# A recomputed opening schedule for batch 0: GpSimd held from H to dH, weight low parts on two engines, batch 1's first sums moved ahead of the main loop

## The chip, the core and the metric

The kernel runs on one core of a Trainium2 chip. A core has five engines that each work through their own queue in order: TensorE (PE, matrix products, with a separate row PEld for its weight loads), VectorE (DVE), ScalarE (ACT), GpSimd (POOL) and SyncE (SP, here only a DMA queue). Engines wait for one another by semaphores. The metric is the device time of one execution in microseconds, lower is better. Three timed runs of the kernel before gave 304.07, 304.18 and 304.26 us.

## The reference

Four batches of 12480 rows with 128 channels, 32 inducing vectors, and a gated feed-forward of width 2048 behind the attention:

```python
def mab(q, kv):
    s = scale * (q @ kv.transpose(0, 2, 1))
    s = s - s.max(-1, keepdims=True)
    a = np.exp(s)
    a /= a.sum(-1, keepdims=True) + 1e-09
    return a @ kv
h = mab(I, x)                  # 32 x 128 for each batch
y = mab(x, h)                  # 12480 x 128 for each batch
...
u = y @ w_in                   # 128 -> 2048
g = u * np.clip(u + 3.0, 0.0, 6.0) / 6.0
out = g @ w_out                # 2048 -> 128
```

Every output row depends on the whole batch only through `h`, a 32 x 128 matrix. Once `h` (called H below) is known, the kernel turns both weight matrices into small tables, and each row is finished with these tables.

## The kernel before

**Stages.** A batch is cut into seven groups of rows: six of 2048 (16 tiles of 128) and a rest of 192. Stage A goes over the groups: x is loaded by DMA issued from POOL (`load_x`, L140), cast to bf16 (L299), transposed on PE (L310), copied from PSUM (`xT`, L317), multiplied with the inducing vectors (scores, L323), exponentiated on ACT (L333), and the weighted sums of x are accumulated on PE in one PSUM bank (`hnd`, `a_agg`, L360), while DVE adds up the weights (`dacc`, `a_sum`, L375 and L377). Stage C follows: H is `hnd` over its denominator (L464), HT its transpose (L474), then HTb and HTl (its bf16 high and low part, L479 and L484), W, Wd and dH (sums and differences of its columns, L489 to L502). From these come the table G of `w_in` with H (`gp`, L514, three products for each of 16 blocks; the third one needs `w_in_l`, the low part of `w_in`), hs and L and BD (L567 to L603), and for batch 0 sixteen products dpm of `w_in` with dH (L613), each squared to a bf16 tile sq (L623 to L628) and multiplied with `w_out` into one PSUM bank cp (L639), from which Cq is read (L652 and L654). Stage B, the main loop, goes over 25 chunks of a batch: for each chunk features TF (bp, L816, and an exponential, L829) and TD (L844, which needs a tile d spread over the partitions by a DMA from SP, L804), the product with BD that opens the output bank (L855), 16 products with Cq (L874), and on DVE the scaling and evacuation (L894).

**What overlaps.** Batch 0 has nothing to hide behind: its stages A and C are laid out by a table, `ORDER`, of some 200 tokens. A token issues one step, and its position fixes the order on that step's engine; `:A`, `:D`, `:P` name ACT, DVE or POOL, and `:o` or `:f` the PSUM pool (`psO` with two banks, `psF` with five; a third pool `psH` has one bank, for `hnd`). The other tokens that matter here are: `wi` (cast of half of `w_in` on ACT), `wl` (an eighth of `w_in_l`, `w_low`), `wo` (cast of a quarter of `w_out`), `bk`, `bT`, `bx`, `bs`, `ba` (batch 1's group 0: casts, transposes, copies, scores, exponential), `pe` (the two products ep and pp), `e` and `dk` (their exponentials), `spread` (the DMAs of d), `dp`, `q`, `C` (dpm, square, product into cp), `G` (four blocks of gp), `by` and `bg` (new, see the change). A square is done on ACT in one step, or, where the block is in `BY_DVE`, on DVE in two (copy from PSUM, multiply). The token `made` puts a one-element copy on POOL that reads W, so POOL's queue stands still until W is there; the token `held` does the same with d of chunk 3 and then issues the four loads of batch 1's groups 1 to 4.

**Batch 1 in the loop.** From the first chunk of the main loop on, `a_units` (L379) deals the steps of the next batch's stage A out over the loop at fixed positions between the groups of four products (`bg`, L1049). Batch 1's group 0 is cast, transposed, scored and exponentiated in the opening already; its weighted sums (two halves of eight products) and its `dacc` copy are issued by `a_units` in the loop, and behind the second half `load_next` (L163) issues the load of batch 1's group 5.

Of the kernel before, what the change touches and what calls it, by code (L numbers as in the profile page):

```python
# [9 lines left out]
FP32 = mybir.dt.float32  # L10
# [19 lines left out]
AHEAD = 6  # L30
CASTLEAD = 1.6
SUMG = 5
BY_DVE = (1, 4, 7, 10)


ORDER = """
half s0:o k1.1:P k1.2 k1.0:D a0 warm1:o T1.0:o T1.1:f y0 xT1.0:A g0.0 xT1.1:D g0.1 k2.0:P k2.2
k2.1:D s1:f dx5 T2.0:f a1 dx6 T2.1:f xT2.0:D g1.0 xT2.1:A y1 g1.1 k3.1:D k3.2 dx10 k3.0:D s2:f
T3.0:o dwi a2 T3.1:o xT3.0:A g2.0 y2 dwo g2.1 xT3.1:D s3:f k4.0:D k4.2 k4.1:D warm2:f T4.0:f a3
T4.1:f xT4.0:D g3.0 xT4.1:A y3 g3.1 k5.0:D k5.1:P k5.2 s4:f k6:D T6:f T5.0:o xT6:D a4 T5.1:o  # L40
xT5.0:D s6:f g4.0 xT5.1:A y4 g4.1 dred a6 s5:f bk2:A bk3:P a5 bk0:P bT1:f bk1:P n5 wi0 n6 den
bT0:f dall rD bx1:A g5.0 wl1 bx0:D g5.1 wl2 wi1 g6 bs:f wl3 H htp:o ba wl0 HT HTb wo1:A Wd wl6
warm3:o pe1:of wo0:A HTl pe0:ff wo2:P dk1 G0 dH e1 G1 dk0 wl7 dp9:f e0 dp7:f spread0 dp5:o W q9
dp15:f dp1:o q7 wl4 q5 bp0.0:f C9 q15 made wl5 bp1.0:f C5 q1 C7 dp11:o TF1.0 held dp10:f dp14:f
TF0.0 G2 q10 C1 q14 G3 dp0:f wo3:A hs bp0.1:o q0 C10 C14 C15 dp6:f cmax TF0.1 dp2:f dp8:f C0 q2
TD0 L0:f q8 L1 q6 C8 dp4:o L q11 C2 C6 q4 dp12:f dp13:f dp3:f q12 lt:f sp0:o q13 BD C12 q3 C4
C13 nf0 C11 C3 bp1.1:o Cq rp0:f TF1.1 rp1 r0 warm1:f
""".split()


# [17 lines left out]
def kernel(  # L68
# [8 lines left out]
    nc = tc.nc  # L77
# [31 lines left out]
    with ExitStack() as es:  # L109
# [82 lines left out]
            at = slice(h * F // 2, (h + 1) * F // 2)  # L192
            nc.scalar.copy(w_in_b[:, at], w_in_r[h][:, :].bitcast(FP32))

        def w_low(i):
            lo, hi = i * 256, (i + 1) * 256
            t, at = w_in_r[2 * lo // F], lo % (F // 2)
            nc.gpsimd.tensor_sub(w_in_l[:, lo:hi], t[:, at : at + 256].bitcast(FP32), w_in_b[:, lo:hi])
# [154 lines left out]
        def a_agg(b, g, h):  # L353
            t0, p, n = groups[g]
            st = S[b]
            lo, hi = (0, n // 2) if h == 0 else (n // 2, n)
            if g == 0 and h == 0:
                st["hnd"] = psH.tile([P, 512], FP32, name="hnd", tag="hnd")
            for i in range(lo, hi):
                nc.tensor.matmul(  # L360
                    st["hnd"][:M, :C],
                    lhsT=st[("a1", g)][:p, i * M : (i + 1) * M],
                    rhs=xs[(b, g)][:p, i, :],
                    start=(g == 0 and i == 0),
                    stop=(g == NGR - 1 and i == n - 1),
                )
            if h:
                load_next(b, g)

        def a_sum(b, g):  # L370
# [8 lines left out]
        def a_units(b, when):  # L379
# [121 lines left out]
            nc.vector.tensor_sub(st["dH"][:, 0], shifted(HT, 0, 1, 0), shifted(HT, 2, 0, 2))  # L501
            nc.vector.tensor_sub(st["dH"][:, 1], shifted(HT, 1, -1, 0), shifted(HT, 10, 0, 2))  # L502
# [413 lines left out]
        def first(kind, ix, how):  # L916
# [45 lines left out]
                while held:  # L962
                    load_x(1, held.pop(0))
            elif kind == "made":
                gate("made", S[0]["W"][:, 0, 0, 0:1])
            elif kind == "wi":
                w_in_cast(i)
            elif kind == "wo":
                w_out_cast(i, eng)
            elif kind == "wl":  # L970
                w_low(i)
            elif kind == "bk":
                a_cast(1, 0, ((eng, i, i + 1),))
            elif kind == "bT":
# [4 lines left out]
                a_scores(1, 0, at)  # L979
            elif kind == "ba":  # L980
                a_exp(1, 0)
            elif kind == "dred":
                c_sum(0)
            elif kind == "HTb":
# [338 lines left out]
```

## Time and profile before

| | |
|---|---|
| median of three runs | 304.18 us (304.07 to 304.26) |
| the profiled execution's own time | 304.03 us |
| its span, first to last instruction | 302.3 us |
| PE busy | 285.4 us (94%) |
| DVE, ACT, POOL busy | 237.3, 228.8, 119.0 us |
| H written (L464) | 28.52 to 28.86 us |
| first product with Cq (L874) | 44.73 us |

The opening table covers the time from 0 to 44.7 us, and the main loop the rest. An engine row that is busy says only that the engine had an instruction under way; a PE row of 100% in a stretch means that no gap is seen between its matmuls there. In the timelines each row is a start, a duration, an engine, the source line, the operation with output and inputs, and a count of merged instructions; in square brackets stand the idle time before it and what ended it.

### The profile page before, as it was taken

The page shows a single profiled execution, that of the slowest core. Times are in us where ns is not written, and L with a number is a line of the kernel's source. Part 1 is how long each engine was busy: PE and PEld are TensorE (multiplying, and loading weights), DVE is VectorE, ACT ScalarE, POOL GpSimd, SP SyncE. Part 2 cuts the span into 40 slices and gives each one's busy share as a digit, 9 for nine tenths or more (in the row PEclk, how much of TensorE's full clock was granted, in tenths as well). Part 3 has the DMA queues.
Part 4 walks back from the last instruction along what each step waited for, and adds up shares of the span by engine and source line. Part 5 has one row for each costly group of instructions (what it writes and reads, how often), then busy time and mean ns, then how long its engine had stood idle before and what let it go on. Part 6 is the DMA issues. An engine that isn't in the chain of part 4 may idle for free. (4 is left out here: it accounts for less than half of the span.)

```text
span 302.3 us, 9818 instructions
## 1 busy us (share of the span) xinstructions
PE 285.4 (94%) x3973; PEld 229.0 (76%) x3973; DVE 237.3 (79%) x494; ACT 228.8 (76%) x427; POOL 119.0 (39%) x234
## 2 busy tenths in 40 slices
PE   8989899999998999999998999998799999999992
PEld 3777478988887787887887878777677777777881
DVE  1766898878998588879896787787787787888892
ACT  3788968777878988769698888665687787777760
POOL 8367435411029996000297744000777760000000
PEclk9999999999999999999999999999999999999998
DMA  6999498899867459988657515436553666666753
GB/s 213 426 391 242 104 330 315 274 356 327 297 197 241 130 169 299 360 236 296 194 126 255 177 26 193 161 97 199 187 172 75 189 203 202 197 214 217 218 207 114
DMA packets 25281, 66.69 MB, mean 221 GB/s; under 512 B 3184, under 2 KB 18320, under 8 KB 19344
## 3 DMA queue, kind: packets, MB, share of 16 engines
q1 hardware_dynamic: 18784, 38.36, 39.4%
q0 software_dynamic: 6448, 27.66, 28.6%
q8 instruction: 32, 0.52, 0.7%
q14 instruction: 17, 0.14, 0.1%
HBM read 27.67 MB, written 25.56 MB: 176 GB/s over the span
## 5 line engine op out<-in xcount | busy, mean ns | idle before, releaser
L829 ACT ACTIVATE TF<-bp 128x512 bf16<-128x512 f32 (+1 forms) x200 | 115.7, 589 | 33.7 <-PE bp L816 19.7
L874 PE MATMUL op<-Cq,TF 128*128 128x128 bf16 (+1 forms) x784 | 104.6, 221 | 0.0
L874 PE MATMUL op<-Cq,TD 128*128 128x128 bf16 (+1 forms) x784 | 102.5, 219 | 0.0
L894 DVE TENSOR_TENSOR os<-op,r_all 128x512 f32<-128x512 f32 x96 | 65.9, 687 | 22.8 <-PE op L874 22.2
L844 DVE TENSOR_TENSOR TD<-TF,d 128x1024 bf16<-128x1024 bf16 (+1 forms) x100 | 75.7, 757 | 2.6 <-ACT TF L829 1.5
L816 PE MATMUL bp<-xT,W 128*128 128x512 bf16 (+1 forms) x200 | 74.9, 375 | 2.1 <-DVE nf_all L730 1.0
L874 PEld LDWEIGHTS <-TF 128*128 128x128 bf16 (+1 forms) x784 | 55.1, 98 | 24.4 <-issue 12.9
L874 PEld LDWEIGHTS <-TD 128*128 128x128 bf16 (+1 forms) x784 | 60.4, 98 | 0.2 <-issue 0.2
L855 PE MATMUL op<-BD,nf 128*128 128x512 f32 (+1 forms) x100 | 52.5, 525 | 0.0
L299 ACT CAST xb<-xr 128x512 bf16<-128x512 f32 (+1 forms) x66 | 43.3, 663 | 6.6 <-DMA xr<-in_x_dram 6.6
L317 DVE COPY xT<-pt 128x1024 bf16<-128x1024 bf16 (+1 forms) x50 | 30.3, 609 | 15.3 <-PE pt L310 14.0
L544 POOL TENSOR_TENSOR dg<-G 128x256 f32<-128x256 f32 x48 | 40.6, 846 | 0.0
L543 POOL TENSOR_TENSOR dg<-G 128x256 f32<-128x256 f32 x48 | 31.8, 662 | 13.5 <-ACT sq L551 8.8
L541 POOL COPY gate<-TD 128x1 bf16<-128x1 bf16 x48 | 11.7, 244 | 61.2 <-DVE TD L844 60.5
L551 ACT ACTIVATE sq<-dg 128x512 bf16<-128x512 f32 x48 | 30.2, 632 | 3.0 <-POOL dg L544 2.9
L310 PE MATMUL pt<-ident_b,xb 128*128 128x128 bf16 x392 | 30.4, 219 | 1.7 <-DVE xb L299 1.2
L360 PE MATMUL hnd<-xr,a 128*32 128x128 f32 x384 | 30.9, 226 | 0.0
L310 PEld LDWEIGHTS <-xb 128*128 128x128 bf16 x392 | 23.3, 98 | 5.5 <-DVE xb L299 2.4
L759 PE MATMUL rp<-one,nf 128*128 128x4 f32 (+1 forms) x100 | 26.2, 264 | 0.0
L795 ACT ACTIVATE dk<-pp 128x512 bf16<-128x512 f32 (+1 forms) x28 | 15.6, 557 | 13.6 <-PE pp L781 13.6
L360 PEld LDWEIGHTS hnd<-xr,a 128*32 128x32 f32 x384 | 24.7, 109 | 1.2 <-issue 0.8
L639 PE MATMUL cp<-w_out_b,sq 128*128 128x128 bf16 x256 | 23.7, 219 | 1.9 <-ACT TF L829 1.3
(126 smaller groups left out, 398.5 us busy)
## 6 DMA issues: line engine op xcount, KB each, us to landing
xr<-in_x_dram POOLq DMA_DIRECT2D x23, 1024.0 KB, 7.6
out_dram<-os SPq DMA_DIRECT2D x23, 1024.0 KB, 4.1
d<-dk SPq DMA_DIRECT2D x96, 128.0 KB, 4.4
xr<-in_x_dram POOLq DMA_DIRECT2D x2, 512.0 KB, 4.7
w_in_r<-in_moe_w_in_dram POOLq DMA_DIRECT2D x2, 512.0 KB, 9.7
w_out_r<-in_moe_w_out_dram POOLq DMA_DIRECT2D x4, 256.0 KB, 10.4
out_dram<-os SPq DMA_DIRECT2D x4, 256.0 KB, 3.5
xl<-in_x_dram POOLq DMA_DIRECT2D x4, 96.0 KB, 4.3
```

The costliest lines, as they stand in the source:

```text
L299: eng(xb[:p, lo:hi, :], xs[(b, g)][:p, lo:hi, :].bitcast(FP32))
L310: nc.tensor.transpose(pt[:, (i - lo) * p : (i - lo + 1) * p], xb[:p, i, :], ident_b[:p, :p])
L317: eng(S[b][("xT", g)][:, lo * p : hi * p], pt[:, : (hi - lo) * p])
L360: nc.tensor.matmul(st["hnd"][:M, :C], lhsT=st[("a1", g)][:p, i * M : (i + 1) * M], rhs=xs[(b, g)][:p, i, :], start=(g == 0 and i == 0), st ...
L543: nc.gpsimd.tensor_sub(dg[:, 0], stepped(G2, jb, 0, 1, 0), stepped(G2, jb, 2, 0, 2))
L544: nc.gpsimd.tensor_sub(dg[:, 1], stepped(G2, jb, 1, -1, 0), stepped(G2, jb, 10, 0, 2))
L816: nc.tensor.matmul(st[("bp", c, k)][:, :w], lhsT=st["W"][:, k].rearrange("p m i -> p (m i)"), rhs=st[("xT", g)][:, j * w : (j + 1) * w],)
L829: nc.scalar.activation(st[("x", c)][:, k, :w], bp[:, :w], ACT.Exp, scale=scale)
L844: nc.vector.tensor_mul(u[:, :, :w], t[:, :, :w], d[:, :w].unsqueeze(1).to_broadcast([P, 2, w]))
L855: nc.tensor.matmul(op[:p, : S_ * C], lhsT=st[("nf", g)][:R, j * p : (j + 1) * p], rhs=st["BD"][:R, : S_ * C], start=True, stop=False, skip ...
L874: nc.tensor.matmul(op[:p, s * C : (s + 1) * C], lhsT=T[k][:, s * p : (s + 1) * p], rhs=st["Cq"][:, k, :], start=False, stop=(s == S_ - 1 a ...
L894: nc.vector.tensor_mul(ot[:p, j * S_ : (j + 1) * S_, :], op[:p, : S_ * C].rearrange("p (s c) -> p s c", c=C), r_all[:p, b, c, :S_].unsquee ...
```

## The change

`ORDER` is replaced as a whole. Beside the new order of the steps, these things differ:

- The squares on DVE are blocks 2, 6, 11 (three) where they were 1, 4, 7, 10 (four).
- `w_low` takes an engine: parts 0, 7, 1 and 4 go to DVE (part 0 ahead of H, part 7 between H and HT, parts 1 and 4 between HT and dH), parts 2, 3, 5 and 6 stay on POOL.
- The gate `made` reads the last half of dH, where it read W. Ahead of it POOL has parts 2 and 3; behind it parts 5 and 6 and then `held`. POOL's share of the `w_out` casts (`wo2`) goes to ACT, so ACT has all four.
- `bg` (batch 1's group 0 weighted sums, two halves) and `by` (`a_begin` and the `dacc` copy for it) are issued in the opening: the products between the transpose of H and `pe0`, the copy behind W. In the loop only `load_next(1, 0)` is left of that unit.
- Batch 0's gp takes a bank of `psF` (`G0:f`), since the bank of `hnd` is in use by batch 1's sums.
- `pe1` and `dk1` come much later, so that SP gets four spreads behind `dk0` and the other two behind `dk1`, where it got all six at once.
- `c_tail`, which writes Cq in two instructions, is the same text in both.

```diff
-BY_DVE = (1, 4, 7, 10)
+BY_DVE = (2, 6, 11)
 ORDER = """
-half s0:o k1.1:P k1.2 k1.0:D a0 warm1:o T1.0:o T1.1:f y0 xT1.0:A g0.0 xT1.1:D g0.1 k2.0:P k2.2
-k2.1:D s1:f dx5 T2.0:f a1 dx6 T2.1:f xT2.0:D g1.0 xT2.1:A y1 g1.1 k3.1:D k3.2 dx10 k3.0:D s2:f
-T3.0:o dwi a2 T3.1:o xT3.0:A g2.0 y2 dwo g2.1 xT3.1:D s3:f k4.0:D k4.2 k4.1:D warm2:f T4.0:f a3
-T4.1:f xT4.0:D g3.0 xT4.1:A y3 g3.1 k5.0:D k5.1:P k5.2 s4:f k6:D T6:f T5.0:o xT6:D a4 T5.1:o
-xT5.0:D s6:f g4.0 xT5.1:A y4 g4.1 dred a6 s5:f bk2:A bk3:P a5 bk0:P bT1:f bk1:P n5 wi0 n6 den
-bT0:f dall rD bx1:A g5.0 wl1 bx0:D g5.1 wl2 wi1 g6 bs:f wl3 H htp:o ba wl0 HT HTb wo1:A Wd wl6
-warm3:o pe1:of wo0:A HTl pe0:ff wo2:P dk1 G0 dH e1 G1 dk0 wl7 dp9:f e0 dp7:f spread0 dp5:o W q9
-dp15:f dp1:o q7 wl4 q5 bp0.0:f C9 q15 made wl5 bp1.0:f C5 q1 C7 dp11:o TF1.0 held dp10:f dp14:f
-TF0.0 G2 q10 C1 q14 G3 dp0:f wo3:A hs bp0.1:o q0 C10 C14 C15 dp6:f cmax TF0.1 dp2:f dp8:f C0 q2
-TD0 L0:f q8 L1 q6 C8 dp4:o L q11 C2 C6 q4 dp12:f dp13:f dp3:f q12 lt:f sp0:o q13 BD C12 q3 C4
-C13 nf0 C11 C3 bp1.1:o Cq rp0:f TF1.1 rp1 r0 warm1:f
+half s0:o k1.0:P k1.2 k1.1:D a0 warm2:o T1.0:o T1.1:f y0 xT1.0:A g0.0 xT1.1:D g0.1 k2.1:P k2.2
+s1:f k2.0:D dx5 a1 T2.0:f dx6 T2.1:f y1 xT2.0:A g1.0 xT2.1:D g1.1 k3.0:P k3.2 k3.1:D s2:f dx10
+T3.0:o a2 dwi T3.1:o xT3.0:D g2.0 xT3.1:A y2 dwo g2.1 s3:f k4.1:D k4.2 k4.0:D warm3:f T4.0:f a3
+T4.1:f xT4.0:D g3.0 xT4.1:D g3.1 k5.1:P k5.2 s4:f k5.0:D y3 a4 T5.0:f k6:A T5.1:o y4 xT5.0:A
+g4.0 xT5.1:D g4.1 bk3:A bk2:P T6:o s5:f xT6:D bk1:A bk0:P bT1:f a5 dred s6:f bT0:f a6 wi0 n5
+bx1:D g5.0 bx0:D wl2:P wi1 n6 den g5.1 rD wl0:D g6 wo0:A bs:f dall wl3:P H ba htp:o wl7:D HTb HT
+wo1:A bg0 wl1:D HTl wo2:A Wd bg1 wl4:D wo3:A dH pe0:of G0:f W e0 made dp14:f dp4:f wl5:P dk0
+dp0:f dp11:o by G1 q14 spread0 dp6:o q11 wl6:P G2 q0 C14 q4 bp1.1:f C0 dp7:f TF1.1 q6 C11 dp12:f
+q7 dp3:o q12 held G3 C7 q3 C6 hs C12 bp0.1:f C3 bp0.0:f TF0.1 pe1:of TF0.0 cmax dp8:o TD0 dp5:f
+dk1 dp10:f C4 dp1:f q5 L0:f q10 C5 L1 e1 C10 q1 dp2:f L dp15:f q8 lt:o q2 C1 q15 dp13:f C8 dp9:f
+q13 C15 BD sp0:o q9 C13 C2 nf0 C9 bp1.0:f Cq rp0:f TF1.0 rp1 r0
 """.split()
...
-        def w_low(i):
+        def w_low(i, eng):
...
-            nc.gpsimd.tensor_sub(w_in_l[:, lo:hi], t[:, at : at + 256].bitcast(FP32), w_in_b[:, lo:hi])
+            eng.tensor_sub(w_in_l[:, lo:hi], t[:, at : at + 256].bitcast(FP32), w_in_b[:, lo:hi])
...
-            if h:
+            if h and (b, g) != (1, 0):
                 load_next(b, g)
...
-                if g == 0:
+                if g == 0 and b > 1:
                     us.append((0.0, CASTLEAD + 0.1, lambda: a_begin(b)))
...
                 late = [lambda g=g: summed(g, 0), lambda g=g: summed(g, 1)]
+                if (b, g) == (1, 0):
+                    late = [lambda: load_next(1, 0), lambda: None]
...
-        def c_G3(b, lo, hi):
+        def c_G3(b, lo, hi, how="f"):
...
-                st["gp"] = (psF if b else psH).tile([P, 512], FP32, name="gp", tag="fb" if b else "hnd")
+                st["gp"] = bank(how, [P, 512], FP32, "gp")
...
             elif kind == "made":
-                gate("made", S[0]["W"][:, 0, 0, 0:1])
+                gate("made", S[0]["dH"][:, 1, 1, 0, 0:1])
...
             elif kind == "wl":
-                w_low(i)
+                w_low(i, nc.vector if how == "D" else nc.gpsimd)
...
+            elif kind == "bg":
+                a_agg(1, 0, i)
+            elif kind == "by":
+                a_begin(1)
+                a_sum(1, 0)
...
                 b_dk(0, i)
-                if i and ("d", 0) in S[0]:
+                if i and "spread" in S[0]:
                     spread_rest()
             elif kind == "spread":
                 for c in range(4):
                     b_spread(0, c)
+                S[0]["spread"] = True
                 if ("dk", 1) in S[0]:
                     spread_rest()
...
             elif kind == "G":
-                c_G3(0, 4 * i, 4 * i + 4)
+                c_G3(0, 4 * i, 4 * i + 4, at)
```

## The prediction

> **What bounds the kernel now.** I read the page first, then the busy times by stretch, then the timelines of DVE, ACT, PE and POOL from H (28.86 us) to the first product with Cq (44.73 us).
>
> ```profile
> PE 285.4 (94%) x3973; PEld 229.0 (76%) x3973; DVE 237.3 (79%) x494; ACT 228.8 (76%) x427; POOL 119.0 (39%) x234
> 20.00:30.00 10.00, 9.09 (x168) 7.82 (x165) 6.85 (x15) 8.56 (x14) 6.53 (x10) 1.00 1.35 287
> 30.00:40.00 10.00, 8.67 (x125) 5.57 (x121) 9.13 (x15) 8.56 (x18) 5.33 (x11) 1.00 0.49 114
> 40.00:50.00 10.00, 10.00 (x126) 7.81 (x123) 8.22 (x19) 7.80 (x17) 2.79 (x4) 1.00 1.05 403
> 50.00:60.00 10.00, 10.00 (x165) 9.03 (x163) 9.04 (x15) 7.36 (x14) 5.14 (x9) 1.00 0.73 236
> ```
>
> PE is busy for 94% of the span and shows no gap from 40 to 60 us, so in the main loop a PE instruction taken away is time taken away. From 30 to 40 us it isn't PE: it has 1.3 us of gaps there (8.67 of 10 us), and DVE is the fullest engine. The DVE timeline says why:
>
> ```profile
> 28.52 0.34 DVE L464 TENSOR_SCALAR H<-hnd,rD 32x128 f32<-32x128 f32 x1 [0.39 <-PE hnd L360]
> 29.19 0.22 DVE L474 COPY HT<-htp 128x64 f32<-128x64 f32 x1 [0.34 <-PE htp L469]
> 29.45 0.73 DVE L495 TENSOR_TENSOR Wd<-HT 128x32 bf16<-128x32 f32 x1
> 30.11 0.63 DVE L484 TENSOR_TENSOR HTl<-HT,HTb 128x32 bf16<-128x32 f32 x1
> 30.66 0.94 DVE L501 TENSOR_TENSOR dH<-HT 128x256 bf16<-128x256 f32 x1
> 31.53 0.89 DVE L502 TENSOR_TENSOR dH<-HT 128x256 bf16<-128x256 f32 x1
> 32.34 0.41 DVE L489 TENSOR_TENSOR W<-HT 128x256 bf16<-128x256 f32 x1
> 33.09 0.69 DVE L625 COPY d<-dpm 128x512 f32<-128x512 f32 x1 [0.35 <-PE dpm L613]
> ...
> 34.61 0.69 DVE L625 COPY d<-dpm 128x512 f32<-128x512 f32 x1
> ...
> 43.90 0.56 DVE L652 TENSOR_SCALAR Cq<-cp 128x384 bf16<-128x384 f32 x1 [0.26 <-PE cp L639]
> 44.37 0.34 DVE L654 TENSOR_SCALAR Cq<-cp,half_of 128x128 bf16<-128x128 f32 x1
> ```
>
> From HT on, DVE goes from one instruction to the next; its waits of note are 0.35 us for the first dpm and 0.26 us for the last product into cp. A square costs it 34.61 - 33.09 = 1.52 us, copy and multiply together. And four instructions are slower than their like, as the views by tile show (least, median and longest duration in ns over the four batches):
>
> ```profile
> L495 DVE TENSOR_TENSOR Wd<-HT x4: 184/186/734, 29.5 to 206.3; 128x32 bf16<-128x32 f32 x4
> L484 DVE TENSOR_TENSOR HTl<-HT,HTb x4: 193/193/629, 30.1 to 205.8; 128x32 bf16<-128x32 f32 x4
> L489 DVE TENSOR_TENSOR W<-HT x4: 411/420/421, 32.3 to 205.9; 128x256 bf16<-128x256 f32 x4
> L198 POOL TENSOR_TENSOR w_in_l<-w_in_r,w_in_b x8: 659/670/846, 26.9 to 33.0; 128x256 bf16<-128x256 f32 x8
> ```
>
> Wd and HTl take 734 and 629 ns in batch 0 where the median is 186 and 193; dH takes 943 and 885 ns for a shape that W does in 411. These four run while POOL makes low parts (26.9 to 33.0 us); W ran as POOL waited for it. So POOL's work costs DVE 0.55 + 0.44 + 0.53 + 0.47 = 1.99 us on the way to the first dpm. ACT and PE, meanwhile, wait in turn:
>
> ```profile
> 26.73 1.02 ACT L317 COPY xT<-pt 128x1024 bf16<-128x1024 bf16 x1
> ...
> 28.98 0.60 ACT L333 ACTIVATE a<-s 128x512 fp32r<-128x512 f32 x1 [0.28 <-PE s L323]
> ...
> 31.66 0.60 ACT L795 ACTIVATE dk<-pp 128x512 bf16<-128x512 f32 x1
> ...
> 32.88 1.57 ACT L628 ACTIVATE sq<-dpm 128x512 bf16<-128x512 f32 x3
> ...
> 38.98 2.06 ACT L628 ACTIVATE sq<-dpm 128x512 bf16<-128x512 f32 x4 [0.86 <-PE dpm L613]
> 41.55 1.57 ACT L628 ACTIVATE sq<-dpm 128x512 bf16<-128x512 f32 x3 [0.50 <-PE dpm L613]
> ```
>
> ```profile
> 32.47 1.24 PE L613 MATMUL dpm<-dH,w_in_b 128*128 128x512 bf16 x5 [0.69 <-DVE dH L502]
> ...
> 37.67 0.84 PE L639 MATMUL cp<-w_out_b,sq 128*128 128x128 bf16 x12 [0.46 <-DVE sq L626]
> ...
> 44.73 0.28 PE L874 MATMUL op<-Cq,TF 128*128 128x128 bf16 x2
> ...
> 48.11 0.67 PE L360 MATMUL hnd<-xr,a 128*32 128x128 f32 x8
> ...
> 49.54 0.67 PE L360 MATMUL hnd<-xr,a 128*32 128x128 f32 x8
> ```
>
> ```profile
> L816 PE MATMUL bp<-xT,W 128*128 128x512 bf16 (+1 forms) x200 | 74.9, 375 | 2.1 <-DVE nf_all L730 1.0
> L360 PE MATMUL hnd<-xr,a 128*32 128x128 f32 x384 | 30.9, 226 | 0.0
> ```
>
> ACT stands 0.86 and 0.50 us for dpm, because PE in front of these dpm stands 0.46 us for a square of DVE (37.67). The last square ends at 41.55 + 1.57 = 43.12, and 1.61 us later, with the last product into cp and Cq, comes the first product at 44.73. The opening is thus bounded by DVE, with ACT close behind.
>
> **The change part by part.** *POOL held from H to dH.* Without low parts on POOL, Wd, HTl and the two halves of dH fall to 186, 193 and twice 411 ns: -1.99 us of DVE.
>
> *Low parts on DVE.* No such instruction on DVE is in the trace. Nearest below is W (two inputs from SBUF, 256 elements, 0.41 us), nearest above dH beside a busy POOL (0.94 us). Parts 1 and 4 stand between HT and dH with POOL held, so W's price holds: +0.82 us (up to 1.89). Part 7 falls into the 0.34 us that DVE waits for the transpose in front of HT and overhangs by 0.07; part 0 falls into the 0.39 us in front of H, beside POOL's parts 2 and 3, and may push H by 0.5 us if it is slowed like dH.
>
> *One square less on DVE*: -1.52 us. ACT takes it for 0.49 us (four squares in 2.06 us, one alone 0.60).
>
> *The new dacc copy* behind W. Its row in the loop:
>
> ```profile
> 48.79 0.41 DVE L375 COPY dacc<-a 128x512 f32<-128x512 f32 x1
> ...
> 51.09 1.67 DVE L844 TENSOR_TENSOR TD<-TF,d 128x1024 bf16<-128x1024 bf16 x1
> ...
> 54.49 0.68 DVE L844 TENSOR_TENSOR TD<-TF,d 128x1024 bf16<-128x1024 bf16 x1
> ```
>
> 0.41 us, of which 0.35 us fall where DVE waits for the first dpm today: +0.06. W and this copy, however, now meet POOL's parts 5 and 6, which are let go when dH is written. One of the two may be slowed by the mean of the four differences above, 1.99 / 4 = 0.50 us. TD at 51.09 takes 1.67 us where the next one takes 0.68, so such slowings aren't confined to the opening. I take +0.5 (bounds 0 and 1.0).
>
> [...]
>
> DVE's sum: -1.99 - 1.52 + 0.82 + 0.07 + 0.06 = -2.56, so its queue alone would allow the first product at 42.2, with the 0.5 us at 42.7.
>
> *ACT's queue.* Behind H it holds, beside HTb (0.18 us), 25 instructions where it held 24: thirteen squares, four TF, two dk, two e, three casts of w_out, and the first scores' exponential. Ahead of H, the copy at 26.73 (1.02 us) leaves, and two casts come that I put at 0.49 us each, so that exponential stays at 28.98. Spaced 0.49 us, the last square, the 24th, starts at 28.98 + 0.18 + 23 x 0.49 = 40.43 and ends at 41.03; with the 1.61 us behind it the first product comes at 42.64. This is the floor if ACT never waits. A wait there now costs all of itself, which it doesn't today.
>
> *Where the three engines wait for each other.* dH ends at 29.19 + 0.07 + (32.42 - 29.19) - 1.99 + 0.82 = 31.32 (32.42 today); the first dpm follows at once, in time for ACT, whose seventh instruction is the first square (28.98 + 0.18 + 6 x 0.49 = 32.1). DVE ends W at 31.7 and the copy at 32.1, or 32.6 with the 0.5 us; squares 11 and 6 end at 34.05 and 35.55. On PE, the product C11 waits until 34.1, and dpm 12 behind it reaches ACT at 34.7 where ACT is ready at 34.55. C6 waits until 35.6; behind it stand C12 (four products into cp at the pace of the row at 37.67, 0.07 us each or less, take at most 0.28 us, here 0.22) and bp0.1, whose result comes at 35.6 + 2 x 0.22 + 0.38 = 36.4 (0.375 us is a bp's mean), where ACT's 14th instruction could start at 35.7 with the slip so far. So ACT slips by some 0.75 us, and the first product comes at 42.64 + 0.75 = 43.4: **-1.3 us** for the opening. DVE's wait later for L costs nothing, since ACT is behind. Bounds: -2.1 (ACT never waits), and +0.2 (parts 0, 1 and 4 at the slowed price, 1.06 us in front of dH and 0.5 in front of H, all handed on by C6).
>
> *First sums in the gap.* The sixteen products leave the loop, where they start at 48.11 and 49.54. Eight take 0.67 us with the tail of the last, 0.226 us by the mean of their group; at (0.67 - 0.226) / 7 = 0.064 us each, sixteen are 1.02 us. In the opening they stand between HT and dH, a stretch in which PE has today only warming products and the first eps; with 31.3 - 29.2 = 2.1 us to fill they hide there. Without that cover they would cost 1.02 us again. **-1.02 us**, bounds -1.0 and 0.
>
> *Ahead of H* the table moves casts and copies between engines, but H follows the last products into `hnd`, and the products in front of these on PE are the same ones. PE has 0.9 us of gaps from 20 to 30 us (9.09 of 10), which is the most that the new order could win; part 0 could lose 0.5. I take 0.
>
> *Edits at nothing.* gp in a bank of `psF` leaves three banks in turn for dpm and bp besides cp's, and two of `psO`; hidden by squares on two engines, and up to 0.4 us if PE runs into a taken bank. G2 waits for part 5: 31.3 + 0.19 (the gate) + 0.67 = 32.2, while PE must first issue five dpm at 0.215 us behind 31.4 and G1. Parts 6 and the gate `held` follow at 32.9 on POOL, four microseconds before the tile that `held` reads arrives today (37.09, below). Two of the six spreads go behind dk1, at about 37.3; their tiles are needed by the fifth chunk's TD at 54.49 less 2.3, some 14 us later, against 4.4 us to land at the median of all spreads. The load of batch 1's group 5 keeps its place in the loop. Cq is written in two instructions before and after, so "as a pair" takes nothing away here.
>
> ```profile
> d<-dk SPq DMA_DIRECT2D x96, 128.0 KB, 4.4
> ```
>
> The sum, against the profiled execution (304.03 us; span 302.3 and 1.7 outside it): 304.03 - 1.3 - 1.02 = 301.7. The median of the runs is 0.15 us above that execution, so I forecast 301.9.
>
> **The rivals.** *A, ACT is never kept waiting.* [...] For it speaks that DVE's own queue would allow 42.2; against it that ACT waits twice in the rows above and that C6 has a DVE square in front.
>
> *B, the loop gives the sums back.* If DVE and not PE paces the loop around 50 us, only the opening counts: -1.3, at most -1.4, so 302.8. For it: DVE 9.04 of 10 us from 50 to 60, and TD of 1.67 us. Against: PE 10.00 in the same stretch, and DVE loses the 0.41 us copy there.
>
> *C, the subtractions on DVE cost what the held POOL saves*: the bound +0.2 - 1.02, so 303.4. For it: no such instruction has been seen on DVE. Against: W, the same shape, is 411 to 421 ns in all batches.
>
> *D, slower: batch 1's loads come late.*
>
> ```profile
> 37.09 0.19 POOL L910 COPY seen<-d 128x1 bf16<-128x1 bf16 x1 [3.46 <-DMA d<-dk]
> ...
> 43.71 1.17 POOL L299 CAST xb<-xr 128x512 bf16<-128x512 f32 x2 [4.19 <-DMA xr<-in_x_dram]
> ```
>
> ```profile
> 46.80 0.61 PE L310 MATMUL pt<-ident_b,xb 128*128 128x128 bf16 x8
> ```
>
> The four loads start when d of chunk 3 has landed, 37.09 - 32.26 = 4.8 us behind dk0's end (31.66 + 0.60), and the first cast of what they bring starts 6.6 us later, with 1.17 us for two casts. So batch 1's next transposes can't start before dk0's end + 12.6, 44.9 today, and are due at 46.80, 2.07 behind the first product. With that at 43.4 they are due at 45.5. dk0 now stands behind three casts of w_out, whose last quarter comes last from memory, and behind pp0, which waits on PE for the sixteen sums, which wait for batch 1's exponential. If dk0 ends 0.6 us later than today, PE begins to stall; beyond 0.6 + 2.3 = 2.9 us the kernel is slower than before. At 4 us it is 305.3. Against it: by ACT's count dk0 is the sixth instruction and ends at 28.98 + 0.18 + 5 x 0.49 + 0.60 = 32.2, as today.
>
> *E, nothing is gained.* Both terms vanish: 304.2.
>
> **How the numbers follow.** Forecast 0.43, A 0.20, B 0.12, C 0.10, D 0.12, E 0.03. Range: A's time less 0.6 of the 0.9 us that H could come earlier gives 300.5 at the bottom; the top is C with its slack, 303.9, which leaves out D, E and the tails. Faster or slower means beyond 0.2% (0.6 us), about what a measurement of this kernel can tell from no change: the forecast, A and B are faster, C mostly, D slower: faster 0.80, within 0.2% 0.07, slower 0.13.
>
> **What would show it.** Wd and HTl near 0.19 us and dH twice near 0.41; low parts on DVE near 0.41; the first dpm near 31.4 (32.47); no dacc copy and no `hnd` products for group 0 in the loop; the first product with Cq at 43.4, and every later row earlier by 2.3 us from about 52 us on. The forecast is wrong if PE shows gaps in front of pt between 44 and 52 us (D), if the lead at the first product shrinks over the loop (B), or if ACT's row between 32 and 42 us has no gap (A).

## The result, and the profile after

| | before | after |
|---|---|---|
| median on one chip | 304.21 us (304.07 to 305.2, 6 runs) | 302.27 us (302.12 to 303.13, 6 runs) |
| profiled execution, its span | 304.03, 302.3 us | 302.12, 300.3 us |
| first product with Cq | 44.73 us | 43.68 us |

The ratio is 0.9937 with a 95% interval of 0.992 to 0.9953: faster by 1.9 us, where 301.9 us was forecast. The source is two lines longer behind the edits of `a_units`, so dH's second half is L504 here and was L502.

First a stretch of the changed kernel; columns: length, then PE, weight loads, DVE, ACT and POOL with their instructions, granted clock, DMA share, GB/s.

```profile
30.00:40.00 10.00, 9.75 (x145) 6.56 (x144) 7.53 (x17) 9.30 (x19) 4.31 (x8) 1.00 0.41 102
```

From 30 to 40 us DVE fell from 9.13 to 7.53 us of ten and PE rose from 8.67 to 9.75: DVE no longer sets this stretch by itself, and ACT (8.56 to 9.30) has become the fullest engine beside PE. The DVE timeline of the changed kernel, from part 0 of the low parts to the first square, and then its end:

```profile
27.66 0.50 DVE L198 TENSOR_TENSOR w_in_l<-w_in_r,w_in_b 128x256 bf16<-128x256 f32 x1
...
29.47 0.23 DVE L476 COPY HT<-htp 128x64 f32<-128x64 f32 x1 [0.49 <-ACT HTb L481]
29.61 0.41 DVE L198 TENSOR_TENSOR w_in_l<-w_in_r,w_in_b 128x256 bf16<-128x256 f32 x1
29.94 0.18 DVE L486 TENSOR_TENSOR HTl<-HT,HTb 128x32 bf16<-128x32 f32 x1
30.05 0.18 DVE L497 TENSOR_TENSOR Wd<-HT 128x32 bf16<-128x32 f32 x1
...
30.82 0.42 DVE L504 TENSOR_TENSOR dH<-HT 128x256 bf16<-128x256 f32 x1
31.16 0.42 DVE L491 TENSOR_TENSOR W<-HT 128x256 bf16<-128x256 f32 x1
31.49 0.42 DVE L375 COPY dacc<-a 128x512 f32<-128x512 f32 x1
32.41 0.69 DVE L627 COPY d<-dpm 128x512 f32<-128x512 f32 x1 [0.50 <-PE dpm L615]
...
39.64 0.28 DVE L595 TENSOR_SCALAR L<-lp 32x128 f32<-32x128 f32 x1 [1.16 <-PE lp L584]
...
41.42 0.68 DVE L605 TENSOR_TENSOR BD<-lt,one_f 128x512 fp32r<-128x512 f32 x1
42.21 0.69 DVE L732 CUSTOM_DVE_ANT_0 nf<-e,sp 128x512 fp32r<-128x512 f32 x1
...
42.90 0.56 DVE L654 TENSOR_SCALAR Cq<-cp 128x384 bf16<-128x384 f32 x1
```

HTl and Wd are back at 0.18 us and dH at 0.42, a low part on DVE costs 0.41 with POOL held and 0.50 beside a busy POOL. Two things are new: HT stands 0.49 us until HTb, which also reads htp, is done, since the table now issues HTb first, and the end of the opening (BD, nf, Cq) is one queue on DVE with hardly a gap (0.11 us, in front of nf). The timelines of POOL, ACT and PE of the changed kernel:

```profile
31.30 0.66 POOL L912 COPY made<-dH 128x1 bf16<-128x1 bf16 x1 [2.61 <-DVE dH L504]
...
36.77 0.19 POOL L912 COPY seen<-d 128x1 bf16<-128x1 bf16 x1 [3.56 <-DMA d<-dk]
```

```profile
28.77 0.60 ACT L333 ACTIVATE a<-s 128x512 fp32r<-128x512 f32 x1 [0.18 <-PE s L323]
...
33.67 0.60 ACT L831 ACTIVATE TF<-bp 128x512 bf16<-128x512 f32 x1 [0.18 <-PE bp L818]
...
36.27 1.08 ACT L831 ACTIVATE TF<-bp 128x512 bf16<-128x512 f32 x2 [0.53 <-PE gp L516]
...
41.33 1.08 ACT L630 ACTIVATE sq<-dpm 128x512 bf16<-128x512 f32 x2 [0.36 <-PE lt L600]
```

```profile
29.42 1.15 PE L360 MATMUL hnd<-xr,a 128*32 128x128 f32 x16 [0.48 <-ACT a L333]
...
31.36 0.81 PE L615 MATMUL dpm<-dH,w_in_b 128*128 128x512 bf16 x3
...
39.68 0.59 PE L615 MATMUL dpm<-dH,w_in_b 128*128 128x512 bf16 x2
40.20 0.48 PE L600 MATMUL lt<-L,sel 32*128 32x128 f32 x2
...
43.68 0.31 PE L876 MATMUL op<-Cq,TF 128*128 128x128 bf16 x2
...
46.76 0.39 PE L702 MATMUL ep<-xT,HTb 128*32 128x512 bf16 x4
47.14 0.38 PE L818 MATMUL bp<-xT,W 128*128 128x512 bf16 x1
```

W and the copy of dacc, which were to be slowed by POOL's parts, take 0.42 us each. It was POOL that stood: its one-element gate began beside W and took 0.66 us, to just behind the end of the copy (31.49 + 0.42), where the like gate on d takes 0.19. In u1 below, where W is there and the copy isn't, the gate takes 0.32.

The rest of the way is seen on the rows that evacuate the chunks, the first and the last but one, before (L894) and after (L896):

```profile
46.05 0.69 DVE L894 TENSOR_TENSOR os<-op,r_all 128x512 f32<-128x512 f32 x1 [0.62 <-PE op L874]
...
295.53 0.69 DVE L894 TENSOR_TENSOR os<-op,r_all 128x512 f32<-128x512 f32 x1
```

```profile
45.02 0.69 DVE L896 TENSOR_TENSOR os<-op,r_all 128x512 f32<-128x512 f32 x1 [0.58 <-PE op L876]
...
293.63 0.69 DVE L896 TENSOR_TENSOR os<-op,r_all 128x512 f32<-128x512 f32 x1
```

The lead is 1.03 us at the first chunk and 1.90 at the end: 1.05 us come from the opening (44.73 - 43.68) and 0.85 from the sums that left the loop.

### The profile page after: what moved, and what is told of

Read it like the earlier page. It is cut to its first block, busy times and chain, and to the rows that moved or that the text cites. A ratio compares the mean times of both kernels' runs of the same rounds, so it can differ in the third digit from the quotient of the medians.

```text
span 300.3 us, 9798 instructions
## 1 busy us (share of the span) xinstructions
PE 283.7 (94%) x3950; PEld 228.2 (76%) x3971; DVE 234.6 (78%) x496; ACT 228.5 (76%) x429; POOL 116.0 (39%) x229
## 5 line engine op out<-in xcount | busy, mean ns | idle before, releaser
L896 DVE TENSOR_TENSOR os<-op,r_all 128x512 f32<-128x512 f32 x96 | 65.9, 687 | 22.7 <-PE op L876 22.2
L846 DVE TENSOR_TENSOR TD<-TF,d 128x1024 bf16<-128x1024 bf16 (+1 forms) x100 | 74.6, 746 | 2.5 <-ACT TF L831 1.5
L818 PE MATMUL bp<-xT,W 128*128 128x512 bf16 (+1 forms) x183 | 68.4, 375 | 2.1 <-DVE nf_all L732 1.0
L317 DVE COPY xT<-pt 128x1024 bf16<-128x1024 bf16 (+1 forms) x52 | 31.5, 611 | 15.1 <-PE pt L310 13.8
```

Of the source, the lines that this page charges most:

```text
L317: eng(S[b][("xT", g)][:, lo * p : hi * p], pt[:, : (hi - lo) * p])
L818: nc.tensor.matmul(st[("bp", c, k)][:, :w], lhsT=st["W"][:, k].rearrange("p m i -> p (m i)"), rhs=st[("xT", g)][:, j * w : (j + 1) * w],)
L846: nc.vector.tensor_mul(u[:, :, :w], t[:, :, :w], d[:, :w].unsqueeze(1).to_broadcast([P, 2, w]))
L896: nc.vector.tensor_mul(ot[:p, j * S_ : (j + 1) * S_, :], op[:p, : S_ * C].rearrange("p (s c) -> p s c", c=C), r_all[:p, b, c, :S_].unsquee ...
```

## The experiments

The kernel before ran beside each of them, with medians of 304.12 to 304.24 us.

| kernel | median (range, runs), us | ratio (95% interval) | dH ends | first dpm | first product |
|---|---|---|---|---|---|
| h1_hold_only | 303.02 (302.69 to 303.15, 10) | 0.9947 (0.993 to 0.9964) | 30.42 | 31.30 | 43.57 |
| u2_no_hold | 302.27 (302.0 to 303.37, 10) | 0.994 (0.9921 to 0.9959) | 31.50 | 31.55 | 43.91 |
| s1_sums_only | 303.69 (303.35 to 305.09, 10) | 0.9979 (0.9958 to 1.0) | 32.57 | 32.62 | 45.35 |
| c1_hold_and_sums | 303.55 (303.18 to 304.97, 10) | 0.9985 (0.9974 to 0.9996) | 30.68 | 32.43 | 45.13 |
| u1_sums_in_loop | 304.0 (302.49 to 305.32, 10) | 0.9977 (0.9951 to 1.0003) | 31.27 | 31.32 | 44.79 |
| u3_loop_and_warm | 303.13 (302.6 to 304.42, 10) | 0.9977 (0.9959 to 0.9994) | 31.20 | 31.26 | 43.59 |
| p1_all_pool | 302.29 (301.94 to 303.69, 5) | 0.9931 (0.9894 to 0.9968) | 30.45 | 31.11 | 43.44 |
| v1_tail | 302.29 (301.96 to 302.36, 4) | 0.9941 (0.9924 to 0.9957) | 31.31 | 31.43 | 43.69 |
| v2_head_tail | 301.8 (301.73 to 301.94, 4) | 0.9927 (0.991 to 0.9943) | 30.69 | 30.78 | 43.31 |
| v3_nine | 301.8 (301.58 to 303.22, 5) | 0.9925 (0.989 to 0.9959) | 30.55 | 30.64 | 43.15 |
| v4_nine_pool | 304.1 (302.73 to 304.47, 10) | 0.9965 (0.9941 to 0.9989) | 30.54 | 30.83 | 43.70 |

The last three columns are from each profile (end of the row dH, starts of the first rows dpm and op with Cq), in us.

### POOL held, alone and taken away

h1_hold_only is the kernel before with POOL's queue alone reordered:

```diff
-g5.0 wl1 bx0:D
+g5.0 wl0 wl1 bx0:D
...
-ba wl0 HT HTb wo1:A Wd wl6
+ba HT HTb wo1:A Wd
...
-wo2:P dk1 G0 dH e1 G1 dk0 wl7 dp9:f
+dk1 G0 dH made e1 G1 dk0 wo2:P wl4 dp9:f
...
-q7 wl4 q5
+q7 wl5 q5
...
-q15 made wl5 bp1.0:f
+q15 wl6 wl7 bp1.0:f
...
-gate("made", S[0]["W"][:, 0, 0, 0:1])
+gate("made", S[0]["dH"][:, 1, 1, 0, 0:1])
```

> The kernel before with POOL's queue alone reordered: four low parts ahead of H, then the gate on dH, then wo2 and the other four. Theory (DVE is the bound of the opening and loses 1.99 us to POOL): Wd and HTl at 0.19, dH at 0.41 twice, first dpm at 30.6 to 31.0 where it is 32.47, first product with Cq 1.2 to 2.0 us earlier, total 302.2 to 303.0. Rival: ACT and PE take over as the bound (casts and exponentials stand in front of the first squares), 0.3 to 0.6 us faster than before.

Its rows on DVE and, after them, on PE:

```profile
30.00 0.42 DVE L502 TENSOR_TENSOR dH<-HT 128x256 bf16<-128x256 f32 x1
```

```profile
31.30 1.24 PE L613 MATMUL dpm<-dH,w_in_b 128*128 128x512 bf16 x5
```

dH ends at 30.42, 2.00 us earlier than before, and the first product with Cq comes 1.16 us earlier. The first dpm (30.6 to 31.0 expected) and the first product fall a little short of the expectation. Where the 2.00 go is on PE: pe0, pe1, G0 and G1 stand in front of the first dpm, which starts 0.88 us after dH is there. This one reordering of POOL gives the changed kernel's whole gain in the opening (1.05).

u2_no_hold takes the gate out of the changed kernel:

```diff
-W e0 made dp14:f
+W e0 dp14:f
```

> The changed kernel without the gate on dH: POOL goes on with low parts 5 and 6 while DVE makes HT to dH. Theory (POOL's low parts slow DVE instructions by some 0.45 us each): HTl, Wd and low parts 1 and 4 take 0.6 to 0.9 us, dH ends 0.8 to 1.3 us later than 31.24, first product with Cq 0.3 to 0.9 us later, total 0.3 to 0.9 us slower than the changed kernel. Rival: PE's sums and G0 set the first dpm anyway (31.36) and DVE has 0.5 us to spare there, so under 0.2 us.

```profile
29.48 0.81 DVE L198 TENSOR_TENSOR w_in_l<-w_in_r,w_in_b 128x256 bf16<-128x256 f32 x1
```

Of DVE's instructions between HT and dH only this one, part 1, was slowed (0.81 for 0.41). The first product comes 0.23 us later and the median is the same, so the rival is the nearer one, though not for its reason: dH ends only 0.26 us later (31.50), and the first dpm comes 0.19 later. In the new table the gate guards little, because only two parts are left behind it; h1 shows what holding POOL is worth with eight.

### The sums, in the opening and in the loop

s1_sums_only is the kernel before with batch 1's first sums, and the copy of dacc, in the opening (with gp in a bank of psF, and load_next(1, 0) alone left of the unit in the loop, as in the change):

```diff
-warm3:o pe1:of
+bg0 bg1 pe1:of
...
-spread0 dp5:o W q9
+spread0 dp5:o W by q9
```

> The kernel before with batch 1's first sums and dacc copy moved into the opening alone (and gp in a psF bank). Theory: the loop wins 0.83 us; the opening loses 0 to 0.5, since ep and pp for both groups and G0 stand behind the sums, which wait for batch 1's exponential: 0.3 to 0.9 us faster than before. Rival: the sums fill a gap that was free, and the copy the 0.35 us that DVE waits: the full 0.83 to 1.0 us.

The first product comes 0.62 us later, and at the fourth chunk the lead is +0.13 us (it ends at +0.33): up to there the sums save 0.75 us in the loop and cost 0.62 in the opening. There they wait for batch 1's exponential and hold back the ep and pp products, for which ACT stands 0.68 us (its first dk starts at 31.52), so that ACT's first square starts at 33.44 where it was 32.88. The first dpm isn't held back: it follows dH at once (32.62, 32.47 before), and dH is as much later as H is in this execution, 0.14 us.

c1_hold_and_sums has the edits of h1_hold_only and of s1_sums_only, still in the old table, and no others.

> The kernel before with both h1 and s1: POOL held and sums in the opening, old table otherwise. If the two add up: 302.3 to 302.6 (-1.2 and -0.55), as fast as the changed kernel, and the new table's dealing of parts and squares has brought nothing. If the sums stand in front of the first dpm, which h1 has at 31.30 with dH at 30.42 already waiting for PE: first product 0.6 to 1.0 us later than in h1 (43.57), total 302.6 to 303.0, and the new table is needed to hold both.

The PE timeline of c1:

```profile
29.76 1.14 PE L360 MATMUL hnd<-xr,a 128*32 128x128 f32 x16 [0.48 <-ACT a L333]
...
32.43 1.29 PE L615 MATMUL dpm<-dH,w_in_b 128*128 128x512 bf16 x5
```

dH is written at 30.68, but sums, pe0, pe1, G0 and G1 keep PE until 32.43, ACT comes to its first square at 33.42 (32.36 in h1), and the first product comes 1.56 us after h1's: more than the sums save, and more than either case expected. Hold and sums don't add in the old table. In the new one pe1, its two exponentials and G1 come behind the first dpm, which starts at 31.36 with the same sums ahead of it, and the first square at 31.91; that is what the new order is good for, as far as these two tables show (moving these steps alone wasn't tried).

u1_sums_in_loop is the changed kernel with sums and copy back in the loop, where the unit is that of before:

```diff
-wo1:A bg0 wl1:D HTl wo2:A Wd bg1 wl4:D
+wo1:A wl1:D HTl wo2:A Wd wl4:D
...
-dp11:o by G1
+dp11:o G1
```

> The changed kernel with batch 1's first sixteen sums and the dacc copy put back into the main loop. Theory: PE paces the loop there, so the loop gives back the 0.83 us that the leads of the opening products show (1.06 us ahead at the first chunk, 1.87 at the third), and the opening keeps its time, since its first dpm waits for dH at 31.24: 0.8 to 1.0 us slower than the changed kernel, 1.0 faster than before. Rival: the sums hold up the opening (they wait 0.48 us for batch 1's exponential, with pe0, G0 and the first dpm behind them), so without them the opening is shorter by 0.3 to 0.5 us and the whole is only 0.4 us slower than the changed kernel.

The median is 304.0 us, nearly the whole gain gone, and in the profile the first product comes at 44.79, 1.1 us later than with the sums. Neither theory has that. The stretches of u1, and then of the changed kernel, show what it was:

```profile
28.00:30.00 2.00, 1.34 (x26) 0.82 (x23) 1.43 (x7) 1.85 (x6) 0.72 (x1) 1.00 0.53 75
30.00:32.00 2.00, 1.48 (x19) 0.78 (x20) 1.60 (x7) 2.00 (x5) 0.67 (x2) 0.96 0.00 0
32.00:34.00 2.00, 1.78 (x30) 1.32 (x30) 1.18 (x2) 1.47 (x4) 0.90 (x2) 0.50 0.27 48
34.00:36.00 2.00, 2.00 (x18) 1.23 (x16) 1.58 (x3) 1.05 (x2) 0.00 (x0) 0.69 0.87 202
```

```profile
32.00:34.00 2.00, 1.95 (x38) 1.51 (x38) 1.45 (x3) 1.82 (x5) 1.21 (x2) 1.00 0.26 45
```

Without the sums PE has 1.18 us of gaps from 28 to 32 us, and then its granted clock halves for some 3.4 us. The old table had warming products (`warm3`) in this place; the new one has the sums, which do their work. The ten runs agree: the two with a mean granted clock of 0.998 took 302.49 and 302.66 us, the eight with 0.983 to 0.992 took 303.68 and more. The first two are only 0.2 and 0.4 us above the changed kernel's median, about where the rival had it (0.4). No such run was profiled, so how early the opening without sums ends at a full clock is seen only with warming products in their place, in the next kernel. u3_loop_and_warm puts the warming products back into u1_sums_in_loop:

```diff
-H ba htp:o wl7:D HTb HT
+H ba htp:o warm3:o wl7:D HTb HT
```

> As u1 (sums in the loop), with three warming products on PE behind the transpose of H, as the kernel before has them. Theory (u1 lost its time to the granted clock, 0.50 from 32 to 34 us, after a stretch with little PE work): the clock stays at 1.00, first product with Cq at 43.2 to 43.8, total 302.9 to 303.4, the loop's 0.8 to 1.0 us more than the changed kernel. Rival: the clock falls all the same, since three products do not fill what sixteen sums did: 304.0.

The clock stays at 1.00 throughout the opening, the first product comes at 43.59, and the lead of the rows of evacuation, 1.12 us at the first chunk (46.05 - 44.93), is 1.17 at the last but one (295.53 - 294.36): the loop gains nothing when the sums stay in it, as the prediction had it. The price of the sums in the loop is thus 1.90 - 1.03 = 0.87 us by the changed kernel and 0.75 by s1, and in the new opening they cost 43.68 - 43.59 = 0.09 more than the warming products do.

### Low parts dealt to two engines

p1_all_pool leaves all eight parts to POOL, four ahead of the gate and four behind it:

```diff
-wl2:P wi1 n6 den g5.1 rD wl0:D g6
+wl2:P wl0:P wi1 n6 den g5.1 rD g6
...
-wl3:P H ba htp:o wl7:D HTb HT wo1:A bg0 wl1:D HTl wo2:A Wd bg1 wl4:D wo3:A dH
+wl3:P wl1:P H ba htp:o HTb HT wo1:A bg0 HTl wo2:A Wd bg1 wo3:A dH
...
-made dp14:f dp4:f wl5:P dk0
+made dp14:f dp4:f wl4:P wl5:P dk0
...
-wl6:P G2
+wl6:P wl7:P G2
```

> The changed kernel with all eight low parts on GpSimd: parts 2, 0, 3 and 1 ahead of the gate, 4, 5, 6 and 7 behind it; DVE subtracts nothing. Nothing is left out. Theory (dealing the parts to two engines is worth little, since what DVE saves by it is what it pays): DVE loses four subtractions of 0.41 us, of which the 0.82 us of parts 1 and 4 and 0.07 of part 7 stand between HT and dH; but GpSimd, whose first part starts at 27.2 us behind the cast of w_in, needs 4 x 0.67 us and so works until 29.9, and HTl and Wd are slowed by about 0.5 us each. dH ends near 31.3 (31.24 in the changed kernel), total within 0.3 us of it: 302.0 to 302.6. Rival (the dealing costs more than it saves): dH ends near 30.5, the first product with Cq comes 0.4 us or more earlier, below 43.3 (43.68), total 301.9 or less. Second rival (the dealing is needed): G0 waits for part 1 or G2 for part 5, the first dpm or the fifth comes later than today, total above 302.6.

POOL and DVE of p1:

```profile
26.95 2.56 POOL L198 TENSOR_TENSOR w_in_l<-w_in_r,w_in_b 128x256 bf16<-128x256 f32 x4 [1.67 <-ACT w_in_b L193]
```

```profile
30.03 0.42 DVE L504 TENSOR_TENSOR dH<-HT 128x256 bf16<-128x256 f32 x1
```

The four parts end at 29.51, just ahead of HTl, so nothing is slowed and dH ends at 30.45, as the rival had it, 0.79 us earlier. Yet the first dpm comes 0.25 us earlier, since PE has sums, pe0 and G0 in front of it until 31.1, the first product 0.24 us earlier, and the end not at all: 302.29 us. In the total, dealing the parts to two engines neither gained nor cost anything that these runs can tell.

### The end of the opening

v1_tail aims at the two waits of ACT in the rows above (0.53 and 0.36 us): bp0.1 and bp0.0 ahead of C6, block 2's dpm and square ahead of L, lt behind dpm 13.

```diff
-G3 C7 q3 C6 hs C12 bp0.1:f C3 bp0.0:f TF0.1
+G3 C7 q3 bp0.1:f bp0.0:f C12 C6 hs C3 TF0.1
...
-C4 dp1:f q5 L0:f q10 C5 L1 e1 C10 q1 dp2:f L dp15:f q8 lt:o q2 C1 q15 dp13:f C8 dp9:f
-q13 C15 BD sp0:o q9 C13 C2 nf0 C9
+C4 dp2:f q5 L0:f dp1:f q10 C5 L1 e1 q2 C10 q1 dp15:f L q8 C1 dp13:f q15 lt:o C2 C8 dp9:f
+q13 BD sp0:o C15 q9 nf0 C13 C9
```

> The changed kernel with the order changed in two places: bp0.1 and bp0.0 ahead of C6, and dpm 2 with its square on DVE ahead of L, lt behind dpm 13. Theory (ACT sets the end of the opening, and its waits of 0.53 us at 36.27, for bp behind C6, and 0.36 us at 41.33, for dpm 13 behind lt and L, are handed on in full): last square 0.5 to 0.9 us earlier, first product with Cq at 42.8 to 43.2, total 301.4 to 301.8. Rival: DVE, which has L, a square, BD, nf and Cq one behind the other from 39.64, sets the end: under 0.2 us won.

ACT of v1:

```profile
41.98 0.60 ACT L630 ACTIVATE sq<-dpm 128x512 bf16<-128x512 f32 x1 [0.54 <-PE dpm L615]
```

Both waits went and another came, for dpm 9, which still stood behind lt on PE: no gain. It isn't L that makes lt late, as the expectations of v3 have it: in v1 L is written at 40.13, and lt starts at 40.63, 0.31 us behind the dpm in front of it. v2_head_tail adds to v1_tail three edits at the head: HT ahead of HTb, the second half of the sums behind the first four dpm, and one cast of `w_out` on POOL.

```diff
-wl7:D HTb HT wo1:A bg0 wl1:D HTl wo2:A Wd bg1 wl4:D wo3:A dH
+wl7:D HT HTb wo1:A bg0 wl1:D HTl wo3:A Wd wl4:D dH
...
-dp0:f dp11:o by G1
+dp0:f dp11:o bg1 by G1
...
-wl6:P G2
+wl6:P wo2:P G2
```

> v1 with the head changed too: HT ahead of HTb (HT waits 0.49 us for HTb now), the second half of the sums behind the first four dpm, one w_out cast back on POOL behind part 6. Theory (ACT's queue of 25 is the length of the opening, and the first dpm waits for PE's sums): dH at 30.8, first dpm at 30.9 (31.36), ACT one cast shorter, first product 0.4 to 0.7 us earlier than v1, total 300.8 to 301.3. Rival: part 5 and the gate let go earlier collide with W and the copy, or C11 waits for the cast on POOL: no faster than v1.

dH ends at 30.69 and the first dpm starts at 30.78, both some 0.6 us earlier than in the changed kernel; 0.37 of that reaches the first product (43.31), and the median is 301.8, a gain of 0.5 us where 1.0 to 1.5 were expected. Which of the three edits gave it wasn't tried. v3_nine then takes v2's dpm 9 out from behind lt:

```diff
-dp13:f q15 lt:o C2 C8 dp9:f q13 BD sp0:o C15
+dp13:f q15 C8 dp9:f q13 lt:o C2 BD sp0:o C15
```

> The kernel of v2_head_tail with the ninth block's dpm ahead of lt on PE (and part of the products into cp and BD behind it). Nothing is left out. Theory (the opening's end is set by ACT's wait of 0.54 us for dpm 9, which stands behind lt and so behind L on DVE): the wait goes, the last square ends 0.4 to 0.5 us earlier, the first product with Cq comes near 42.9 (43.31 in v2_head_tail), total 301.3 to 301.5 (301.80). Rival (DVE sets the end: L, BD, nf and Cq follow one another on it and on PE): ACT is done earlier, but the first product comes no earlier than 43.2, total 301.7 or more.

ACT, DVE and PE of v3:

```profile
38.71 2.70 ACT L630 ACTIVATE sq<-dpm 128x512 bf16<-128x512 f32 x5
```

```profile
39.33 0.28 DVE L595 TENSOR_SCALAR L<-lp 32x128 f32<-32x128 f32 x1
41.07 0.69 DVE L605 TENSOR_TENSOR BD<-lt,one_f 128x512 fp32r<-128x512 f32 x1 [1.47 <-PE lt L600]
41.69 0.69 DVE L732 CUSTOM_DVE_ANT_0 nf<-e,sp 128x512 fp32r<-128x512 f32 x1
...
42.38 0.56 DVE L654 TENSOR_SCALAR Cq<-cp 128x384 bf16<-128x384 f32 x1
```

```profile
40.55 0.48 PE L600 MATMUL lt<-L,sel 32*128 32x128 f32 x2
```

ACT's last square now ends at 41.41, 1.00 us earlier than in the changed kernel, and ACT waits nowhere in its last five squares. The first product follows only 0.53 us earlier (43.15): Cq comes straight behind nf, nf behind BD, and BD waits 1.47 us for lt, which on PE now stands behind dpm 9. L, written at 39.61, isn't late; its product lt is, at 40.55. So the rival held from lt on: with ACT out of the way, lt on PE and BD, nf and Cq on DVE set the end. By medians v2 and v3 are 0.5 us below the changed kernel, with intervals that overlap with its own.

v4_nine_pool is v3_nine with the four low parts moved to POOL as in p1_all_pool.

> The kernel of v3_nine with all eight low parts on GpSimd as in p1_all_pool. Nothing is left out. Theory (in this order ACT sets the opening, and a dH that is ready earlier is worth little): within 0.2 us of v3_nine. Rival (dH earlier is handed on): if dH ends 0.5 us earlier than in v3_nine, the first product with Cq comes 0.3 us or more earlier, total 0.3 us or more below v3_nine.

Neither theory held. PE of v4:

```profile
34.25 0.38 PE L641 MATMUL cp<-w_out_b,sq 128*128 128x128 bf16 x4 [0.20 <-POOL w_out_b L202]
```

The quarter of `w_out` that POOL casts now stands behind eight parts, the product C11 waits for it (34.25, 33.70 in v3), and the first product comes 0.55 us later than in v3 although dH is as early. Its profiled execution also lost 2.2 us near 98 us: a TD takes 1.60 us there (0.69 in the changed kernel), PE stands 0.59 us more, and the clock is halved behind it (last section), as in c1, whose profiled execution lost 1.3 us near 218. So of these two the profiles are read only for the openings. v4's quickest run, 302.73 us, is 1.15 above v3's quickest; 0.55 + 0.59 = 1.14 would explain that, but that run wasn't profiled.

## Why the prediction held, and where it didn't

**Right: what POOL's low parts cost DVE.** Wd, HTl and dH came down as forecast (to 0.18, 0.18 and 0.42 us), and h1 shows that holding POOL moves dH's end by 2.00 us, 0.14 of which H brings along (28.38 for 28.52): 1.86 for the 1.99 forecast.

**Right: dH, and the order behind it.** 31.24 for 31.32, first dpm 31.36 for 31.4. What the sum hadn't is that PE and not dH was next to set the first dpm: in p1 dH is 0.79 us earlier and the dpm 0.25. So the sums hide in the opening only up to dH's own time. That the first dpm came when it was forecast is in part luck: PE came free for it 0.1 us after dH was there. No gain is seen from one DVE square less and the parts on two engines: the new table without the sums has its first product at 43.59 (u3), the old one with POOL held at 43.57 (h1). But these two tables differ in more, and the square, which the sum for DVE priced at 1.52 us, wasn't tried alone.

**Mis-sized: the opening, -1.3 forecast, -1.05 measured.** The term that failed is ACT's slip: 0.75 us, all of it up to the wait behind C6. Up to there the working held: ACT's 14th instruction behind H, the TF that waits for bp0.1, starts at 36.27, where 36.4 was forecast. From there ACT was to go on without a wait, which would have put its last square at 36.27 + 10 x 0.49 = 41.17; it started at 41.33 + 0.48 = 41.81. Nearly all of these 0.64 us are lost in front of the square at 41.33. It needs dpm 13, which on PE stands behind the products lp, dpm 2, dpm 15 and lt, and PE shows no gap from 37 to 41 us. So it is PE's queue that keeps ACT waiting there, and the prediction had no term for it.

Its sentence that DVE's wait for L costs nothing, since ACT is behind, isn't what failed: L waits 1.16 us for lp and is written at 39.92, but lt starts at 40.20, 0.31 us behind the dpm in front of it, and keeps that distance in v1, v2 and v3, where L had been there for 0.51 to 0.95 us.

Counted from the start, without waits the last square would have been at 28.77 + 0.18 + 23 x 0.49 = 40.22, so the slip was 1.59 us for 0.75. The three waits in the rows (0.18, 0.53 and 0.36) are 1.07 of it. Each costs 0.11 more, because an instruction takes 0.60 us by itself and 0.49 in a row; the last 0.19 is spread over the casts and short waits. An earlier start by 0.21 (28.77 for 28.98) and a shorter way from the last square to the product (43.68 - 42.41 = 1.27 for 1.61) gave 0.55 back; the prediction foresaw neither. v3 bears this out: with dpm 13 and dpm 9 ahead of lt ACT is done 1.00 us earlier, and the first product moved by 0.53, because then BD waits for lt.

**Mis-sized: the sums, -1.02 forecast, about -0.85 measured.** The price on PE was right: in the kernel before, each half took 0.51 us from its first product to the next instruction (48.11 to 48.62 and 49.54 to 50.05, below). But in the changed kernel bp comes 0.38 us after ep has started (47.14 - 46.76), where the sums came after 0.32, and pt at 47.75 comes 0.24 us after the products ahead of it, where 0.11 is usual, as DVE's copy of xT from the bank ends at 47.70. These 0.06 + 0.13 = 0.19 us were hidden behind the sums before.

```profile
48.62 0.39 PE L816 MATMUL bp<-xT,W 128*128 128x512 bf16 x1
...
50.05 0.28 PE L874 MATMUL op<-Cq,TF 128*128 128x128 bf16 x2
```

**The 0.5 us for W and the copy didn't come**: POOL was the one to stand (0.66 us for its gate), so the upper of the two values for DVE was the wrong one. Beside POOL's low parts DVE took longer, 0.81 us for part 1 in u2 and 0.50 for part 0, where 0.41 is usual, and one of POOL's own four took 0.85 where their median is 0.67. The gate took 0.66 us here and 0.32 in u1 and in v4. What decides which of the two engines stands, and for how long, these runs don't show.

**The rivals.** A (ACT never waits: 304.18 - 2.1 - 1.02 = 301.1 us) fell by ACT's waits of 0.18, 0.53 and 0.36 us. B fell: the lead grows in the loop from 1.03 to 1.90. C fell: a low part on DVE takes 0.41. D fell: the tile that `held` reads is seen at 36.77 (37.09 before), and the one short wait in front of pt, 0.13 us at 47.75, is for DVE's copy and not for a load.

## What to carry to other kernels

Before dealing work to more engines, look at what a busy engine does to another's few instructions on the critical path: here, keeping POOL's subtractions out of a 3 us stretch gave 1.2 us by the medians. A moved step is worth its price only if the queue that it joins has room up to the point where something else is due: two edits worth 1.2 and 0.5 us gave 0.6 together until the order behind them was changed as well. And before filler on PE is removed, see whether it held the clock up: in u1, without sums or warming products, the granted clock was 0.50 from 32 to 34 us; in u3, with the warming products, 1.00. An engine's queue must be counted with what the other engines' queues put in front of it: the wait that the forecast missed was ACT's, but its cause was the order on PE.

## What the runs showed of the hardware

A halved clock came after gaps of PE shorter than the time that it lasted. In u1 no single gap of PE between 28 and 32 us is over 0.6 us, and they sum to 1.18. In c1 and in v4 the same happened where the next batch begins (stretches of c1, then of v4):

```profile
216.00:218.00 2.00, 1.40 (x18) 0.89 (x17) 1.30 (x3) 1.97 (x5) 2.00 (x4) 0.96 0.90 268
218.00:220.00 2.00, 2.00 (x14) 1.32 (x14) 0.97 (x3) 1.13 (x3) 1.41 (x4) 0.50 0.64 140
220.00:222.00 2.00, 2.00 (x24) 1.88 (x22) 0.52 (x1) 1.16 (x3) 1.33 (x3) 0.69 0.09 14
```

```profile
98.00:100.00 2.00, 2.00 (x30) 1.84 (x30) 0.21 (x1) 1.24 (x4) 2.00 (x5) 0.50 0.55 126
```

If the clock was either whole or halved at each moment, 0.96, 0.50 and 0.69 over three stretches of 2 us make 0.16 + 2.00 + 1.24 = 3.40 us at half speed, in u1 and in c1 alike. PE wasn't idle ahead of the drop: in u1 it was busy for 2.82 of the 4 us from 28 to 32. Nor does the sum of the gaps decide. The kernel before has 0.71 + 0.85 = 1.56 us of them from 214 to 218 us, more than u1's 1.18, and keeps a clock of 1.00:

```profile
214.00:216.00 2.00, 1.29 (x15) 0.98 (x12) 2.00 (x4) 0.58 (x2) 2.00 (x4) 1.00 0.47 197
216.00:218.00 2.00, 1.15 (x16) 0.74 (x17) 1.34 (x4) 1.97 (x5) 2.00 (x5) 1.00 1.00 348
```

It is the same work at which c1's profiled execution dropped, with the same two gaps (1.30 and 0.49 us before, 1.28 and 0.49 in c1). What decides it, these runs don't show.
